# Batch 0's tail loads moved from ScalarE's DMA queue to SyncE's, in a fused attention and MLP-mixer kernel

## The chip, the core and the metric

The kernel runs on one core of a Trainium2 chip. The metric is the device time of one launch in microseconds (us), lower being better; it is given as the median of several runs. A profile of one of the executions is used for everything that is said about single instructions. "Queue" below means the instruction queue of an engine from which DMAs are issued: SyncE's (SP) or ScalarE's (ACT).

## The reference

Two blocks follow each other. The first is a linear attention without softmax, with 8 batches, 8 heads, 576 positions and a head size of 64; the second is a mixer over positions and channels with model width 512 and hidden width 2048. Everything goes in and out as float32.

```python
kv  = einsum('bhsd,bhse->bhde', k, v)            # 64x64 per head
out = einsum('bhsd,bhde->bhse', q, kv)
rms = sqrt(mean(out*out, axis=-1) + 1e-6)
x   = (out / rms * g_norm)                       # then heads joined: [8, 576, 512]

a1  = alpha1 * x + beta1
tok = einsum('ts,bsd->btd', w_tok, a1)           # 576x576 over positions
u   = x + lam * tok
a2  = alpha2 * u + beta2
ch  = maximum(a2 @ w_ch1, 0) @ w_ch2             # 512 -> 2048 -> 512
y   = u + lam * ch
```

## The kernel before

The kernel is one long straight program for all engines. A small planner in the kernel's own Python (`Prog`) writes its order. Every operation is handed to `P.op` with a cost for each engine that could run it, what it reads and writes, and a priority `pri` (smaller is more urgent). `schedule` (L105) then plays the program through with these costs and fixes which engine does what and in which order; `synchronize` and `emit` turn this into instructions and semaphore waits. An operation with `kind="L"` is a load: loads start strictly in the order of their priority, and among equals in the order in which they were written (`in_order`, L132). The planner believes that each load takes its `dma_us` one after the other on a single pipe, plus 2.0 us (L244 to L246). When TensorE has nothing to do in the plan before the first channel matmul, the planner fills in a dummy matmul on the tile `hot` (`dummy`, L290; L931).

Each batch has 576 positions, handled as 512 "main" positions (four chunks of 128) and a "tail" of 64. So q, k and v of one batch come in two ways:

- `load_main` (L499) brings 1 MB, the 512 main positions of all heads, into one of six staging buffers `st`, in pieces of 1 KB that are contiguous in memory. For batch 0, v is brought as two halves of four heads each.
- `load_tail` (L509) brings the last 64 positions of all heads, 128 KB in pieces of 256 B, into `kvft` (k in its lower half of the partitions, v in the upper) or `qft`.

`round_in` (L530) casts what has come into the matmul's type: the mains into `qr`, `kr` and `vr`, the tails into `krt`, `vrt` and `qrt` (L399 on ACT or L400 on DVE; all casts go through one helper). `kv` (L587) multiplies k by v: for batch 0 it does the four main chunks of heads 0 to 3, then those of heads 4 to 7, with the tail's chunk (c = 4, tiles `vrt` and `krt`, L598) last in each sum, so no sum of k times v is complete without the tails. `qtr` (L629) transposes q; L580 is its matmul for the mains, L635 for the tail of batch 0. `norm_first` (L711) is the attention of batch 0: matmuls L723 and L732 give its outputs transposed, ACT squares them (L726, L735), and 40 matmuls with two output columns each add the squares up (L717). The same line L580 then also computes the output with g applied.

`token_weights` (L981) transposes w_tok (L996), after POOL has cast it; `token_sums` (L1007, L1014) and `tok` (L764, L771) follow, then `ut` (L799) and the channel matmuls `ch1` (L838) and `ch2` (L858), which fill the rest of the program. While batch b is in its channel matmuls, the loads, attention and token mixing of later batches are woven in.

All loads are issued by SP, with the exception of batch 0's three tails and of six small parameter vectors (L884 to L891). Those are issued by "AQ", which the planner treats as a queue of its own and which in fact is ACT's instruction queue. The loads' order in `load(0)` is q, k, v first half, v second half (SP), then the tails of q, k, v (ACT's queue); after them SP goes on with w_tok (L893, L896), the four loads of w_ch1 (L1029) and batch 1.

Of the kernel before, what the change touches and what calls it, by code (L numbers as in the profile page):

```python
# [402 lines left out]
def bass_transnormer_attn__then__resmlp_affine_kernel(  # L403
# [15 lines left out]
    with ExitStack() as stack:  # L419
# [3 lines left out]
        def sb(name, shape, dt):  # L423
            return stack.enter_context(nc.sbuf_tensor(name, shape, dt))
# [14 lines left out]
        kvft = sb("kvft", [128, NH, DH], F32)  # L439
        qft = sb("qft", [128, NH, DH], F32)  # L440
# [58 lines left out]
        def load_main(n, src, b, eng, pri, parts=1):  # L499
            i = held[n, b] = stage()  # L500
            nh = NH // parts
            for x in range(parts):
                P.op({eng: 0.6}, lambda e, _, x=x: e.dma_start(
                    st[:, i].rearrange("p (h r) -> p h r", h=NH)[:, nh * x:nh * x + nh],
                    src[b, nh * x:nh * x + nh, 0:512, :].rearrange("h (p c) d -> p h (c d)", c=4)),
                    w=[("st", i, 2 * x // parts + y) for y in range(2 // parts)], dma_us=2.8 / parts,
                    pri=pri, kind="L")

        def load_tail(n, tile, src, b, lo, eng, pri):  # L509
            key = n + "ft" + (str(b % 2) if n == "q" else "")  # L510
            P.op({eng: 0.4}, lambda e, _: e.dma_start(
                tile[lo:lo + 64, :, :], src[b, :, 512:576, :].rearrange("h s d -> s h d")),
                w=[key], dma_us=0.9, pri=pri, kind="L")

        def load(b, pri):
            P.tag = "load.%d" % b
            aq = "AQ" if b == 0 else "SP"
            load_main("q", q, b, "SP", pri)
            load_main("k", k, b, "SP", pri)
            load_main("v", v, b, "SP", pri, 2 if b == 0 else 1)  # L520
            if b == 0:
                load_tail("q", qft, q, 0, 0, aq, pri)
            load_tail("k", kvft, k, b, 0, aq, pri)
            load_tail("v", kvft, v, b, 64, aq, pri)
            if b % 2 == 0 and b:
                load_tail("q", qft, q, b, 0, aq, pri)
            if b % 2 == 0 and b or b == 1:
                load_tail("q", qft, q, b | 1, 64, aq, pri)

        def round_in(b, pri):  # L530
            P.tag = "round_in.%d" % b
# [348 lines left out]


        load(0, -1000)
        for j, src in enumerate((moe_lam, moe_alpha1, moe_beta1)):
            P.op({"AQ": 0.3}, lambda e, _, j=j, s=src: e.dma_start(  # L884
# [3 lines left out]
            pri=-1100)  # L888
        for j, src in enumerate((moe_alpha2, moe_beta2)):
# [5 lines left out]
            pri=-800, kind="L")  # L895
# [15 lines left out]
             pri=-999)  # L911
        P.op(D, lambda e, _: e.tensor_copy(out=identr[:], in_=ident[:]), r=["ident"], w=["identr"],
             pri=-999)
# [155 lines left out]
        tok(0, -390)  # L1069
        ut(0, -390)  # L1070
        load(1, -190)
        round_in(1, -195)
        for key in [("sqt", i) for i in range(5)] + ["e1", "whi"]:
# [9 lines left out]
        for b in range(NB):  # L1083
            B = 100.0 * b
            more, more2 = b + 1 < NB, b + 2 < NB
            n0 = len(P.ops)
            ch1(b, B, 35)
            if first[0] is None:
                first[0] = P.ops[n0]
            if more2:  # L1090
                load(b + 2, B + 12)
            if more:
                norm(b + 1, B + 1)
                tok(b + 1, B + 36)
                if more2:
                    round_in(b + 2, B + 40)
                ut(b + 1, B + 45)
            if more2:
                kv(b + 2, B + 55)
                qtr(b + 2, B + 60)  # L1100
            ch2(b, B + 40, 55)
# [32 lines left out]
```

## Time and profile before

The median is 398.33 us over four runs (397.03 to 399.62). The profiled execution took 398.92 us; its span from first to last instruction is 397.0 us, so 1.9 us lie around the span.

| | before |
|---|---|
| span | 397.0 us |
| mean granted TensorE clock | 0.953 |
| TensorE matmul (PE) busy | 378.2 us, 95% |
| VectorE (DVE) busy | 232.2 us, 58% |
| ScalarE (ACT) busy | 173.8 us, 44% |
| GpSimd (POOL) busy | 81.6 us, 21% |
| moved by DMA on SP's queue | 47.08 MB in 45760 packets |
| moved by DMA on ACT's queue | 0.40 MB in 1608 packets |

How to read the views used below. The *chain of waits* follows the last instruction back to what released each step; a line gives start, length and what it was. The *waits* add up how long an engine sat idle for which releaser, as total, number and longest. The *timeline* gives start, length, engine, line, operation, `out<-in`, shape and count of merged instructions, and in brackets the idle time ahead of them and its releaser. The *table by windows* gives for each stretch of time the busy time of each engine with its number of instructions in brackets, the granted TensorE clock (1.00 is full), the share of DMA time and GB/s. In the names, `ps` is the accumulator memory, PE a matmul and PEld its weight load. "To landing" is the time from issuing a DMA to the release of what waits for it.

### The profile page before, as it was taken

Reading aid. Unit: us, or ns where it says so; the run is one execution under the profiler, and the core shown is the slowest. Engines: PE = TensorE matmul, PEld = TensorE weight load, DVE = VectorE, ACT = ScalarE, POOL = GpSimd, SP = SyncE. Lnnn points to the kernel's source line nnn. Section 1 sums busy time; section 2 is a strip of 40 time slices with the busy share of each in tenths; the row PEclk is TensorE's granted clock in tenths of the full one; section 3 lists DMA queues with packets and bytes.
Section 4 is the critical chain, followed back from the end, with each engine's and each line's share of the span. In section 5 each row is a group of like instructions: output and inputs, shape, how many; then the busy total and the mean of one; then the engine's idle time right before and its main releaser. Section 6 shows DMA issues by size and latency. Waiting matters only on the chain.

```text
span 397.0 us, 5549 instructions
## 1 busy us (share of the span) xinstructions
PE 378.2 (95%) x2240; PEld 234.6 (59%) x2271; DVE 232.2 (58%) x383; ACT 173.8 (44%) x300; POOL 81.6 (21%) x61
## 2 busy tenths in 40 slices
PE   8789997999989999899999999999999999999994
PEld 4469554646878556545686566555775554547641
DVE  6340689796698839954893669374826482710021
ACT  3332763784597225631574126612662147106500
POOL 5210248152016004300350022201420133000000
PEclk9865598999999999999999999999999999999998
DMA  8995698999792912740100011002000210020021
GB/s 248 325 382 173 151 364 267 242 278 308 220 278 83 288 54 75 228 124 35 72 2 2 26 54 53 0 2 79 28 2 0 79 54 0 2 79 28 0 79 54
DMA packets 47393, 47.83 MB, mean 120 GB/s; under 512 B 13885, under 2 KB 38469, under 8 KB 47240
## 3 DMA queue, kind: packets, MB, share of 16 engines
q1 hardware_dynamic: 45760, 47.08, 37.8%
q10 hardware_dynamic: 1608, 0.40, 0.5%
q8 instruction: 18, 0.29, 0.3%
q14 instruction: 7, 0.06, 0.1%
HBM read 38.04 MB, written 9.44 MB: 120 GB/s over the span
## 4 chain that ended last, share of the span: by engine, by line
PE 85%; DVE 7%; DMA 4%; issue 1%; ACTq 1%; ACT 1%
PE ps L858 31%; PE ps L838 29%; PE ps L771 11%; PE ps L584 4%; DMA kvft<-in_v_dram 4%; PE ps L598 2%; PE ps L717 2%; PE ps L799 2%; DVE vr L400 1%; DVE yn L698 1%; PE ps L580 1%; DVE ht L824 1%; PE ps L996 1%; DVE small L686 1%; DVE kr L400 1%
## 5 line engine op out<-in xcount | busy, mean ns | idle before, releaser
L838 PE MATMUL ps<-a2t,w 128*128 128x320 bf16 (+1 forms) x759 | 145.1, 331 | 3.7 <-ACT ht L823 2.4
L858 PE MATMUL ps<-w,ht 128*128 128x512 bf16 x561 | 137.5, 381 | 0.5
L838 PEld LDWEIGHTS ps<-a2t,w 128*128 128x128 bf16 x768 | 73.3, 98 | 44.9 <-ACT ht L823 2.9
L823 ACT ACTIVATE ht<-ps 128x512 bf16<-128x512 f32 (+1 forms) x111 | 72.0, 649 | 54.0 <-PE ps L838 53.4
L858 PEld LDWEIGHTS ps<-w,ht 128*128 128x128 bf16 x576 | 54.7, 98 | 59.5
L704 POOL TENSOR_TENSOR xm<-yn,g_bc 128x512 f32<-128x512 f32 x28 | 45.0, 1606 | 186.2 <-DVE yn L698 185.6
L866 DVE TENSOR_TENSOR xm<-ps,xm 128x512 f32<-128x512 f32 x32 | 22.1, 690 | 56.2 <-PE ps L858 54.5
L779 DVE TENSOR_TENSOR xm<-ps,xm 128x512 f32<-128x512 f32 x32 | 21.8, 690 | 40.7 <-PE ps L771 39.4
L771 PE MATMUL ps<-rt,wt 128*128 128x512 bf16 x155 | 41.8, 390 | 0.3
L684 ACT ACTIVATE sq<-ps 128x512 f32<-128x512 f32 (+1 forms) x35 | 20.7, 592 | 47.8 <-PE ps L584 47.5
L598 PE MATMUL ps<-vr,kr 128*128 128x128 f32 (+1 forms) x128 | 36.9, 382 | 2.9 <-DVE vr L400 2.9
L808 ACT ACTIVATE a2t<-ps,cols 128x512 bf16<-128x512 bf16 (+1 forms) x16 | 12.4, 826 | 47.6 <-PE ps L799 47.6
L584 PE MATMUL ps<-kvc,qt 128*128 128x128 f32 x112 | 32.9, 387 | 0.0
L686 DVE TENSOR_REDUCE small<-sq 128x8 f32<-128x512 f32 (+1 forms) x35 | 23.7, 676 | 10.3 <-ACT sq L684 10.1
L584 PE MATMUL ps<-identr,qr 128*128 128x128 f32 x112 | 29.6, 362 | 0.0
L598 PEld LDWEIGHTS ps<-vr,kr 128*128 128x128 f32 x128 | 26.1, 214 | 5.0 <-DVE vr L400 4.8
L701 DVE TENSOR_TENSOR rt<-yn,ge 128x512 bf16<-128x512 f32 x28 | 26.7, 954 | 0.4
L771 PEld LDWEIGHTS ps<-rt,wt 128*128 128x128 bf16 x160 | 15.8, 100 | 18.5 <-issue 1.6
L698 DVE TENSOR_TENSOR yn<-ps,small 128x512 f32<-128x512 f32 (+1 forms) x35 | 24.0, 685 | 0.5
L584 PEld LDWEIGHTS ps<-kvc,qt 128*128 128x128 f32 x112 | 22.3, 199 | 2.3
L584 PEld LDWEIGHTS ps<-identr,qr 128*128 128x128 f32 x112 | 21.3, 200 | 0.6
L399 ACT ACTIVATE qt<-ps 128x512 fp32r<-128x512 f32 x25 | 14.8, 595 | 7.0 <-PE ps L584 6.9
(122 smaller groups left out, 371.0 us busy)
## 6 DMA issues: line engine op xcount, KB each, us to landing
st<-in_q_dram SPq DMA_DIRECT2D x8, 1024.0 KB, 5.9
st<-in_k_dram SPq DMA_DIRECT2D x8, 1024.0 KB, 8.3
st<-in_moe_w_ch_dram SPq DMA_DIRECT2D x8, 1024.0 KB, 12.7
out_dram<-xm SPq DMA_DIRECT2D x32, 256.0 KB, 2.3
st<-in_v_dram SPq DMA_DIRECT2D x7, 1024.0 KB, 10.7
ht<-in_moe_w_tok_dram SPq DMA_DIRECT2D x1, 1152.0 KB, 13.4
st<-in_v_dram SPq DMA_DIRECT2D x2, 512.0 KB, 11.0
out_dram<-xtl SPq DMA_DIRECT2D x8, 128.0 KB, 2.3
```

The lines of the kernel that those rows point to most:

```text
L584: return e.matmul(t.flat()[:, 128 * pr:128 * pr + 128], a(), m(), start=start, stop=stop)
L598: return e.matmul(t.flat()[:, at:at + w], a, m, start=(c == 0), stop=(c == 4))
L686: P.op({"DVE": dve_us(512)}, lambda e, _: e.tensor_reduce(out=small[rows, s4], in_=sq[rows, s2], axis=AX.X, op=ALU.add), r=[("sq", s2)], w ...
L698: P.op({"DVE": dve_us(512)}, lambda e, _: e.tensor_tensor(out=yn[rows, s3, :].rearrange("p (r h d) -> p r h d", r=4, h=2), in0=heads(t, b, ...
L701: P.op({"DVE": dve_us(512), "POOL": pool_us(512)}, lambda e, _: e.tensor_tensor(out=rto, in0=yn[rows, s3, :], in1=ge1[rows, :], op=ALU.mul ...
L704: P.op({"POOL": pool_us(512)}, lambda e, _: e.tensor_tensor(out=hview(x), in0=hview(yn[rows, s3, :]), in1=g_bc[rows, None, :].to_broadcast ...
L771: return e.matmul(t.flat(), wt[:, sc, col:col + 128], rt[:, sc, :] if sc < 4 else rtt[:], start=(sc == 0), stop=(sc == 4))
L779: P.op({"DVE": dve_us(512)}, lambda e, _: e.tensor_tensor(out=x, in0=t.flat(rows), in1=x, op=ALU.add), r=[t, xkey(b, c)], w=[xkey(b, c)], ...
L823: return e.activation(dst, src(), ACT.Relu)
L838: return e.matmul(o, w1[:, dj, 128 * fj:128 * fj + 128], m, start=(dj == 0), stop=(dj == 3))
L858: P.op({"PE": 0.216}, lambda e, _: e.matmul(t.flat(), ht[:, fj, 128 * c:128 * c + 128], w2[:, fj, :], start=(fj == 0), stop=(fj == 15)), r ...
L866: P.op({"DVE": dve_us(512)}, lambda e, _: e.tensor_tensor(out=x, in0=t.flat(), in1=x, op=ALU.add), r=[t] + keys, w=keys, pri=p - 2)
```

## The change

Batch 0's three tail loads go to SP's queue, like those of all other batches. Because loads start in the order in which they are written, they are issued after v's second half and ahead of w_tok. Their order among themselves becomes k, v, q instead of q, k, v. Nothing else is edited; the planner runs again on the changed list.

```diff
         def load(b, pri):
             P.tag = "load.%d" % b
-            aq = "AQ" if b == 0 else "SP"
             load_main("q", q, b, "SP", pri)
             load_main("k", k, b, "SP", pri)
             load_main("v", v, b, "SP", pri, 2 if b == 0 else 1)
-            if b == 0:
-                load_tail("q", qft, q, 0, 0, aq, pri)
-            load_tail("k", kvft, k, b, 0, aq, pri)
-            load_tail("v", kvft, v, b, 64, aq, pri)
-            if b % 2 == 0 and b:
-                load_tail("q", qft, q, b, 0, aq, pri)
+            load_tail("k", kvft, k, b, 0, "SP", pri)
+            load_tail("v", kvft, v, b, 64, "SP", pri)
+            if b % 2 == 0:
+                load_tail("q", qft, q, b, 0, "SP", pri)
             if b % 2 == 0 and b or b == 1:
-                load_tail("q", qft, q, b | 1, 64, aq, pri)
+                load_tail("q", qft, q, b | 1, 64, "SP", pri)
```

## The prediction

> **What bounds the kernel now.** I read the page first: TensorE is busy for 378.2 of 397.0 us, and after 80 us for 307.34 of 317, so only the first 80 us hold much that a load could change. Then I read the chain of waits from 0 to 60 us, since all that the diff touches happens there.
>
> ```profile
> 4.50 15.07 DMA kvft<-in_v_dram
> 19.59 1.43 DVE vrt L400
> ...
> 21.07 0.74 PE ps L598 x4
> 21.80 0.67 PE ps L635 x4
> 22.47 2.00 PE ps L723 x4
> 24.48 2.00 PE ps L948 x2
> 26.48 1.80 PE ps L717 x8
> ```
>
> Batch 0's v tail, issued by ACT's queue at 4.50, lands at 19.57. Its cast ends at 21.0, and only then can the last four matmuls of k times v run. From there the chain is TensorE almost without a break until 52.9. But 15.07 us on the chain is not what can be won: TensorE worked through most of it. The timeline of TensorE shows how much was idle:
>
> ```profile
> 14.89 1.30 PE L948 MATMUL ps<-xm,ones 1*128 1x512 f32 x2
> 16.12 1.22 PE L598 MATMUL ps<-vr,kr 128*128 128x256 f32 x8
> 17.18 1.04 PE L931 MATMUL ps<-hot 128*128 128x512 bf16 x4
> 21.07 0.74 PE L598 MATMUL ps<-vrt,krt 128*128 128x256 f32 x4 [2.85 <-DVE vrt L400]
> ```
>
> The main chunks of k times v are issued by 17.18; what follows until 21.07 is four dummies and 2.85 us of idleness. Third, the table by windows, cut at the places where the granted clock changes (columns: PE, PEld, DVE, ACT, POOL, clock, DMA share, GB/s):
>
> ```profile
> 8.47:11.88 3.41, 2.17 (x12) 1.22 (x10) 0.90 (x3) 1.63 (x3) 0.00 (x0) 1.00 1.15 284
> 11.88:15.29 3.41, 3.41 (x13) 3.01 (x14) 1.54 (x5) 1.23 (x2) 0.00 (x0) 0.50 1.12 337
> 15.29:18.70 3.41, 2.93 (x14) 1.39 (x13) 0.99 (x3) 0.60 (x1) 1.59 (x2) 1.00 1.02 317
> 18.70:22.12 3.42, 1.05 (x8) 0.92 (x8) 1.87 (x4) 0.59 (x4) 2.71 (x3) 1.00 1.05 384
> 22.12:25.53 3.41, 3.41 (x9) 1.87 (x8) 1.39 (x4) 2.46 (x7) 0.00 (x0) 0.50 1.05 387
> ...
> 28.95:32.36 3.41, 3.41 (x17) 3.41 (x18) 0.00 (x0) 0.00 (x0) 0.00 (x0) 0.50 1.08 349
> ...
> 46.01:49.43 3.42, 3.42 (x12) 1.78 (x11) 2.89 (x5) 3.42 (x7) 0.00 (x0) 0.50 1.28 251
> 49.43:52.84 3.41, 3.41 (x17) 1.57 (x16) 2.20 (x5) 1.21 (x2) 0.00 (x0) 1.00 1.04 306
> ```
>
> The window in which TensorE waits for the tail (1.05 of 3.42 us busy) is followed at 22.12 by half clock, and it stays half for 27.3 us, through a stage that TensorE bounds. The wait may therefore cost more than its own length.
>
> **Part 1: when the v tail lands.** The trace's packet records say why it is late. From 9 to 13 us each microsecond holds about 225 packets of 1 KB (k and v mains, SP's queue) and about as many of 256 B (tails, ACT's queue): the two queues take turns packet by packet. From 14 to 16 us the partner is w_tok with packets of 9216 B, and both kinds fall to about 40 per us. The v tail's small packets each wait behind a large one and the last starts at 18.9. In one queue the tails lie ahead of w_tok. By the same records the mains ran at about 330 KB per us before the tails joined; at 8 us 1.30 MB of them were left, 3.9 us at that rate, so their last packet starts at about 11.9 instead of 13.7, and v's second half lands at about 13.1 (it took about 1.1 us from there before, to 14.8). A tail behind a main on SP's queue is seen in batch 2: issued at 69.59, 70.25 and 70.92 and landed 6.3, 6.4 and 6.5 us later, so 0.7 to 0.8 apart. So k tail 13.8, v tail 14.6, q tail 15.3: the v tail is 5.0 us sooner. Its cast took 1.42 us; krt's cast of the same size took 0.41, and POOL was casting w_tok (18.38 to 20.7) during the long one. At 0.41 it is ready by about 15.2.
>
> **Part 2: what of this counts.** With the same order on TensorE the main chunks still end at 17.18, perhaps 0.2 sooner, since k also lands a little sooner but the ACT casts ahead of it set the pace. The next late thing is TensorE itself. Gain: 21.07 − 17.18 = 3.9 us, of which about 1 is dummies that the planner places into its own idle time; if it keeps them all the gain is 2.9. The planner believes the v tail 0.9 us sooner than before, so I take them as gone: 3.9, ends 2.9 and 4.3. The q tail moves the other way: 15.3 instead of 11.4, plus a cast of 0.41. Its matmuls L635 come after the k·v tail, at about 17.9, so 2.2 us of cover remain; without cover it would cost its lateness.
>
> **Part 3: the issues.** ACT loses three issues of 0.73, 0.64 and 0.67 us at 3.06 to 5.17; it waited for q until 6.32 anyway, so 0. SP gains three of about 0.65, ahead of w_tok, of w_ch1 and of batch 1: w_tok is issued at about 7.0 instead of 4.95. Here a rule of the Trainium skill speaks against the change: DMA: Bandwidth & Descriptors, "Issuing engines are not separate DMA queues", says that a second issuing engine does save sequencer time. By it 2.0 us could be lost on everything queued behind. By the row, w_tok took 13.4 us from issue to landing with DMA share at 1.0 and above from 5 to 34 us: it queues for bandwidth, and the bytes ahead of it are no more than before. I take 0, and at worst 2.0 us later landings: w_tok about 20.4, POOL's casts (3.1 us) done by 23.5, first used by L996 at 35.97 before, about 29 after. w_ch1's first load lands at 21.2 and is cast at 34.88; batch 1's q lands at 33.9, cast at 49.60. All covers are 5 us or more.
>
> **Part 4: the clock.** Without the wait, the k·v tail, L635 and L723 follow from 17.2 on, so the window 18.70 to 22.12 holds L723, L948 and the first L717 instead of 1.05 us of work. The fall to half should come at least a window later. By the skill (TensorE: Matmul & The Clock Gate, "What's actually happening") about 3.4 us of sustained activity release the throttle. By that rule the first full window at 22.12 would have done so, and work without the idle gap would never be throttled: the 27.3 us would then shrink by up to half, 13.6 us. The rows say otherwise: windows from 22.12 to 46 are full of PE (3.41 of 3.41) and stay at 0.50. L717's matmuls have two output columns and L948's one input row; they keep the profile's PE busy and evidently do not count. So I let the clock fall in L717's stage again, one window later: 3.4 us at full clock do up to 3.4 us more half-clock work. L717 also waits for ACT's four squares (2.06 us), so I take two thirds, 2.4 us; ends 0 and 13.6, nearest the row of L717.
>
> **Part 5: the new plan.** The list scheduler runs again, and small shifts could change orders anywhere. After 80 us TensorE has 9.7 us of idle in all; I bound this at plus or minus 2 us and take 0.
>
> **Sum.** 3.9 + 2.4 = 6.3 us off the profiled 398.92 gives 392.6; the median lies 0.6 below that execution, so 392.0.
>
> **Rivals.**
> - *Only the wait goes*, and the clock falls at the same piece of work: 398.3 − 3.9 = 394.4. For it: 8.47 to 11.88, with 2.17 us of PE busy, was followed by half clock, so a partly filled window may not be enough. Against: 15.29 to 18.70 was not.
> - *The clock holds*: with L723 and L717 at full speed the stage is short enough to reach real matmuls. 392.0 − 11.2 is the floor, 381; I put it at 383. The full windows at half clock speak against it.
> - *The tails do not come sooner*, because SP cannot issue them: the two v halves took 1.5 us each to issue and one w_ch1 issue took 5.33, so SP is held up while much is outstanding. Two such holds ahead of the v tail: 4.95 + 2 × 5.33 = 15.6, plus the shortest landing of a tail, 2.8, is 18.4, plus the cast 18.8: only 2.3 of the 3.9 us, and nothing of the clock, if the new plan also loses 1 us: 397.
> - *Slower, through DVE beside POOL.* At 57.87 two casts of v (L400) took 5.43 us while POOL ran its multiplies by lam (L1048, 10.36 us for four); a cast of equal shape took 0.68 at 50.95. TensorE then waited, and half clock followed from 63.08 to 66.50. Each further cast that the new plan puts beside POOL costs about 2.0 us if TensorE waits for it, and one more half-clock window 1.7. It decides from a loss of 8.3 us on: four casts and one window are 9.7, giving 401.7. For it: the order there is the planner's free choice. Against: four more is most of what POOL's stretch can hold.
>
> **How the numbers follow.** Forecast 0.42; only the wait 0.27; clock holds 0.11; tails not sooner 0.10; slower 0.10. A measurement of this kernel can tell about 0.5%, 2 us, from no change. The first three are faster by more than that: 0.80. The fourth is within it, 0.10, and the last is slower, 0.10. The range runs from 385, the forecast with 7 us of the clock's unknown, to 397.5, which takes in the wait alone with its lower end, 2.9, and 2 us of a bad plan; out of it are most of the clock case and the slower case, 0.2 in all.
>
> **What would show it.** Right: `kvft<-in_v_dram` landing at 14 to 15.5; the k·v tail matmuls at about 17.2 with no wait for vrt; w_tok landing within 2 us of 18.4; clock 1.00 in the window that ends near 22, then 0.50 during L717. Wrong: an SP issue of the tails later than 12 us; TensorE waiting at L635 for the q tail or at L996 for w_tok; more DVE time of L400 in 57 to 70 us; or 0.50 already ahead of L723.

## The result, and the profile after

The changed kernel takes 383.34 us (median of 12 runs, 381.54 to 394.01) against 398.88 us for the kernel before (median of 17 runs); the ratio is 0.9617, 95% interval 0.9585 to 0.965. That is 15.5 us faster where 6.3 were forecast, and below the range. In 5 of the 18 executions of the changed kernel in this study TensorE's clock was at half for 26 to 31 us and the time 391 to 394 us; this and every later ratio leaves out executions that lie over 1.5% above the fastest of their kernel, as those five do. The profiled execution took 382.95 us, its span is 381.0 us, its mean granted clock 0.982 (before: 397.0 and 0.953). Lines of the kernel after the edit are smaller by 3 than before: L595 is the old L598, L632 the old L635, L714 the old L717, L720 the old L723, L945 the old L948.

The chain of waits from 0 to 55 us of the changed kernel no longer has a tail on it; the same three steps stand as follows (start, length, what):

```profile
16.53 0.56 PE ps L595 x3
17.09 0.56 PE ps L632 x4
17.65 0.89 PE ps L720 x3
```

The tails of k times v, which ran at 21.07, are done by 17.1, and the first attention matmul follows at 17.65 instead of 22.47. In TensorE's timeline the wait for vrt has gone:

```profile
13.99 1.22 PE L595 MATMUL ps<-vr,kr 128*128 128x256 f32 x8
15.10 0.38 PE L595 MATMUL ps<-vrt,krt 128*128 128x256 f32 x1
15.41 1.12 PE L945 MATMUL ps<-xm,ones 1*128 1x512 f32 x2
16.46 0.63 PE L595 MATMUL ps<-vrt,krt 128*128 128x256 f32 x3
```

Main chunks and tails now follow each other; the new plan has put a broadcast (L945) in between. No dummies stand there any more. The table by windows of the changed kernel, in steps of 3.41 us; its granted clock falls at 22.73 and is back at 32.97, so the cuts at 22.51 and 32.75 lie 0.2 us ahead of the changes (PE, PEld, DVE, ACT, POOL, clock, DMA share, GB/s):

```profile
15.68:19.10 3.42, 3.42 (x18) 2.31 (x18) 2.88 (x8) 2.45 (x8) 0.92 (x2) 1.00 1.01 324
19.10:22.51 3.41, 3.41 (x32) 3.41 (x31) 0.99 (x1) 2.43 (x5) 2.60 (x3) 1.00 1.05 387
22.51:25.92 3.41, 3.41 (x20) 3.41 (x18) 0.00 (x0) 0.00 (x0) 0.00 (x0) 0.53 1.05 384
25.92:29.34 3.42, 3.25 (x20) 2.50 (x22) 1.99 (x5) 2.12 (x5) 0.45 (x1) 0.50 1.05 382
29.34:32.75 3.41, 3.25 (x16) 2.23 (x16) 1.71 (x4) 3.20 (x6) 2.10 (x2) 0.50 1.09 350
32.75:36.16 3.41, 3.41 (x22) 1.88 (x21) 2.80 (x5) 1.68 (x3) 0.00 (x0) 0.97 1.09 348
```

Half clock lasts three of these windows, 10.2 us, where it lasted 27.3 before. The two short stretches at half clock of the kernel before, 11.88 to 15.29 and 63.08 to 66.50, are absent too. A second profile of the changed kernel (383.86 us) has the same 10.2 us in two stretches, 18.95 to 22.36 and 25.78 to 32.60, so the place is not fixed.

An account can be made from two numbers of each run. If the clock is either full or half, the time at half is 2 × (1 − mean clock) × span: 37.3 us before, 13.7 after. If TensorE bounds that time, half of it is lost. The span less that half is 378.4 before and 374.1 after. So 11.8 us of the 16.0 in the two profiles are the clock, and 4.3 are the wait and the rest.

One profile is one execution, and that of the kernel before lies high. In the 57 other executions of it whose clock is on record, the time at half was 22.6 to 43.7 us, median 30.0; in the 18 of the changed kernel the median is 13.0. By these medians the clock is worth some 8.5 us of 14, not 11.8 of 16. The stretch at 11.88 in particular is not the change's doing: the profile "gap filled" below has the same program and the same transfers up to there and does not have it.

### The profile page after: what moved, and what is told of

It is laid out like the page before. It is cut to its first block, busy times and chain, and to the rows that moved or that the text cites. A ratio compares the mean times of both kernels' runs of the same rounds, so it can differ in the third digit from the quotient of the medians.

```text
span 381.0 us, 5547 instructions
## 1 busy us (share of the span) xinstructions
PE 367.2 (96%) x2238; PEld 227.5 (60%) x2270; DVE 229.8 (60%) x384; ACT 173.1 (45%) x298; POOL 82.3 (22%) x62
## 4 chain that ended last, share of the span: by engine, by line
PE 83%; DVE 10%; DMA 2%; ACT 2%; issue 1%; SPq 0%
PE ps L855 30%; PE ps L835 28%; PE ps L768 11%; PE ps L581 4%; PE ps L595 3%; DMA st<-in_k_dram 2%; PE ps L796 2%; DVE rt L698 2%; DVE w L1045 2%; PE ps L714 1%; PE ps L577 1%; DVE small L683 1%; DVE ht L821 1%; DVE yn L695 1%; DVE kr L400 1%
## 5 line engine op out<-in xcount | busy, mean ns | idle before, releaser
L835 PE MATMUL ps<-a2t,w 128*128 128x320 bf16 (+1 forms) x760 | 143.4, 329 | 4.3 <-DVE ht L821 2.7
L820 ACT ACTIVATE ht<-ps 128x512 bf16<-128x512 f32 (+1 forms) x107 | 69.5, 650 | 50.1 <-PE ps L835 49.5
L768 PE MATMUL ps<-rt,wt 128*128 128x512 bf16 x155 | 40.1, 380 | 0.3
L595 PE MATMUL ps<-vr,kr 128*128 128x128 f32 (+1 forms) x128 | 34.7, 365 | 0.0
L581 PE MATMUL ps<-kvc,qt 128*128 128x128 f32 x112 | 32.4, 384 | 0.0
L683 DVE TENSOR_REDUCE small<-sq 128x8 f32<-128x512 f32 (+1 forms) x35 | 23.5, 676 | 9.4 <-ACT sq L681 9.3
L698 DVE TENSOR_TENSOR rt<-yn,ge 128x512 bf16<-128x512 f32 x28 | 28.1, 1009 | 0.4
L595 PEld LDWEIGHTS ps<-vr,kr 128*128 128x128 f32 x128 | 24.6, 200 | 1.1 <-DVE vr L400 0.8
L399 ACT ACTIVATE qt<-ps 128x512 fp32r<-128x512 f32 x26 | 15.5, 596 | 8.2 <-PE ps L581 7.8
```

What stands on the lines that cost most here:

```text
L581: return e.matmul(t.flat()[:, 128 * pr:128 * pr + 128], a(), m(), start=start, stop=stop)
L595: return e.matmul(t.flat()[:, at:at + w], a, m, start=(c == 0), stop=(c == 4))
L683: P.op({"DVE": dve_us(512)}, lambda e, _: e.tensor_reduce(out=small[rows, s4], in_=sq[rows, s2], axis=AX.X, op=ALU.add), r=[("sq", s2)], w ...
L698: P.op({"DVE": dve_us(512), "POOL": pool_us(512)}, lambda e, _: e.tensor_tensor(out=rto, in0=yn[rows, s3, :], in1=ge1[rows, :], op=ALU.mul ...
L768: return e.matmul(t.flat(), wt[:, sc, col:col + 128], rt[:, sc, :] if sc < 4 else rtt[:], start=(sc == 0), stop=(sc == 4))
L820: return e.activation(dst, src(), ACT.Relu)
```

## The experiments

The theory T1: the tails' earlier landing removes TensorE's idle gap, and with the gap goes a long stretch of half clock. The rival T2: the edit made the planner write another order, and that order is what is faster. Both could be tried apart, because an op's queue can be changed after the plan is made and before the semaphores are set. The kernel before ran beside each set of runs, with a median of 396.98 to 397.63 us. The edits are shortened to the lines that matter.

**The old plan with the tails on SP, and the new plan with the tails on ACT's queue.**

```diff
 # kernel before
         P.schedule()
+        for o in [o for o in P.sequence if o.kind == "L" and o.eng == "AQ"]:
+            o.eng = "SP"
         P.synchronize()
```

```diff
 # changed kernel
         P.schedule()
+        at = [P.sequence.index(o) for o in tails]      # tails: k, v, q of batch 0
+        for i, o in zip(at, (tails[2], tails[0], tails[1])):
+            P.sequence[i] = o
+            o.eng = "AQ"
         P.synchronize()
```

Expected of the first:

> The order of every compute engine is that of the kernel before, fixed after its planner has run; only batch 0's three tail loads are issued from SP's queue (in the old order q, k, v) instead of ACT's. Theory T1, the transfers and the clock that follows from the idle gap: the v tail lands by about 15.5 us, TensorE doesn't idle ahead of k times v's tail, and half clock comes one window later or more; time 384 to 389, most of the 15 us. Theory T2, the new plan: with the old order only the wait itself is won, 393 to 395, since the 40 two-column matmuls still stand in one block and keep the clock at half up to the token mixing.

Measured: 389.62 us, ratio 0.983 (0.9730 to 0.9931), against 396.98 for the kernel before beside it. Expected of the second:

> The order of every compute engine is that of the changed kernel; only batch 0's three tail loads are issued from ACT's queue again, in the old order q, k, v. T1: the v tail lands at about 19.5 us again, TensorE idles some 4 us, half clock follows the idle window; 395 to 400, nearly all the gain gone. T2: the wait comes back (about 4.5 us) but the new order keeps its part; 387 to 390.

Measured: 400.07 us, ratio 1.0115 (1.0064 to 1.0167), at the upper end of what T1 expected. That is within 2% of the kernel before, and its median is 3.1 us above that of the kernel before beside it (396.98), so the new order alone wins nothing. The transfers alone give 7.4 us, about half of the gain, just above what T1 expected and well below T2's times. T2 falls as the sole cause. Something of it remains, since the two parts together give more than the sum: the new order is good only when the tail is early.

What the order adds shows in two places. The half clock of the old plan on SP lasts 17.1 us (22.8 to 39.8), not 10.2. Its TensorE hardly waits for the tail, and its first and last windows at half clock are these:

```profile
16.30 0.74 PE L598 MATMUL ps<-vrt,krt 128*128 128x256 f32 x4 [0.52 <-DVE vrt L400]
```

```profile
22.80:26.20 3.40, 3.40 (x17) 3.40 (x17) 0.00 (x0) 1.29 (x3) 0.00 (x0) 0.50 1.04 383
...
36.40:39.80 3.40, 3.40 (x13) 1.92 (x12) 2.74 (x4) 3.38 (x8) 0.00 (x0) 0.50 1.21 259
```

And the old plan keeps the stall at batch 1's v casts. DVE's timeline of the old plan on SP:

```profile
48.35 5.44 DVE L400 CAST vr<-st 128x1024 fp32r<-128x1024 f32 x2
```

and of the changed kernel:

```profile
44.20 1.28 DVE L400 CAST vr<-st 128x1024 fp32r<-128x1024 f32 x2
```

The same two casts take 1.28 us where the new order puts them ahead of POOL's multiplies by lam, and 5.44 beside them. In the old plan on SP TensorE waits there and loses the clock once more:

```profile
50.10:53.50 3.40, 1.06 (x5) 0.49 (x5) 3.40 (x2) 1.02 (x2) 3.24 (x3) 1.00 1.05 373
53.50:56.90 3.40, 3.06 (x11) 2.07 (x11) 3.34 (x4) 0.60 (x1) 3.32 (x2) 0.50 1.05 314
```

The two profiles differ by 6.5 us (387.5 and 381.0). Their times at half clock, 23.3 and 13.7, account for 4.8 of it. Most of it arises early: the first channel matmul starts at 57.97 in the kernel before, 48.20 in the old plan on SP and 44.07 in the changed kernel. Which part of the new order keeps the clock up is not tested.

**The wait kept, only the idleness filled.** In the kernel before, 13 dummies stand in the gap:

```diff
         P.schedule()
+        first_tail = min(P.sequence.index(o) for o in KVT)   # KVT: tail matmuls of k times v
+        dummies(first_tail, 13)                              # hot x hot into a free bank
         P.synchronize()
```

> The kernel before, with its plan and its tails on ACT's queue, and 13 more dummy matmuls of 512 columns put on TensorE just ahead of the four tail matmuls of k times v; they add no needed work. The wait for the v tail stays whole, only the idleness goes. T1: the clock stays full past 22 us and the first part of the attention of batch 0 runs at full speed; 3 to 8 us are won, 390 to 395. If idleness is not what takes the clock down: 398 to 399, no change, or up to 1 us slower through dummies that outlast the wait.

Measured: 393.97 us, ratio 0.9932 (0.9873 to 0.999): the smallest gain that T1 expected, 3.0 us below the median of the kernel before beside it. Useless work made the kernel slightly faster. Its table by windows:

```profile
16.90:20.30 3.40, 2.84 (x14) 1.08 (x11) 0.29 (x1) 0.00 (x0) 2.30 (x3) 1.00 1.06 304
20.30:23.70 3.40, 3.08 (x14) 2.02 (x14) 2.11 (x7) 2.31 (x8) 0.74 (x1) 1.00 1.05 388
23.70:27.10 3.40, 3.40 (x29) 3.08 (x28) 1.39 (x2) 0.74 (x2) 0.00 (x0) 1.00 1.05 386
27.10:30.50 3.40, 3.40 (x18) 3.32 (x18) 0.00 (x0) 1.56 (x3) 0.00 (x0) 0.55 1.06 366
```

The k·v tail still comes at 20.61, half a microsecond from where it was, but the clock holds to 27.4 instead of 22.12, and half clock lasts 17.1 us instead of 27.3. Half of the 10.2 us is 5.1; the profiled spans differ by 5.0 (397.0 and 392.0). Over all executions of that set of runs the median time at half clock is 22.8 us with the gap filled, 30.0 in the kernel before and 23.3 in the old plan on SP. So with the order held, filling the gap saves as much half clock as the early tail does: idleness took the clock down, not the lateness of the data.

**The wait put back into the changed kernel, idle and filled.**

```diff
         P.schedule()
+        P.sequence[first_tail].deps.add(wtok_last)     # the load of w_tok's last rows
+        dummies(first_tail, 16)                        # in the second kernel only
         P.synchronize()
```

> The changed kernel with one wait more: the first tail matmul of k times v also waits for the last part of w_tok (lands near 18.7 us in the changed kernel's profile), so TensorE idles about 3.5 us with all tails landed. T1: the idle window brings the half clock back early; 3.5 us for the wait and 4 to 9 us for the clock, 391 to 396. T2: only the wait's own length, 386.5 to 387.5.

> The changed kernel with the same added wait as the one before (the first tail matmul of k times v also waits for the last part of w_tok), and 16 dummy matmuls of 512 columns ahead of the waiting matmul; they add no needed work. The wait is as long, but TensorE doesn't idle through it. T1, the clock follows idleness: about 3.5 to 5 us above the changed kernel, 386 to 389, against the 398.7 of the idle wait. If the lateness itself costs more (work behind it, loads, other engines): near 395 or above.

Measured: idle 398.71 us, ratio 0.999 (0.9912 to 1.0067), somewhat more than even T1 expected; filled 392.06 us, ratio 0.9861 (0.9826 to 0.9897), 3 us more than expected. TensorE's timeline with the idle wait:

```profile
13.71 1.22 PE L597 MATMUL ps<-vr,kr 128*128 128x256 f32 x8
19.85 0.58 PE L597 MATMUL ps<-vrt,krt 128*128 128x256 f32 x1 [4.93 <-DMA ht<-in_moe_w_tok_dram]
```

and with the filled one:

```profile
14.83 3.63 PE L933 MATMUL ps<-hot 128*128 128x512 bf16 x16
19.09 0.38 PE L597 MATMUL ps<-vrt,krt 128*128 128x256 f32 x1 [0.63 <-DMA ht<-in_moe_w_tok_dram]
```

One wait of 5 us brings back everything that the change had gained. Filling it returns about 6 us of that: the profiled spans are 396.9 and 391.5, the times at half clock 33.3 and 21.9, and half of that difference is 5.7. The expectation for the filled kernel missed because I counted only the wait: its trace has half clock in stretches from 21.6, 28.4 and 55.7 us, and 21.9 us in all are 8.2 more than in the changed kernel. Over the executions the medians are 34 us idle and 18.7 filled, against 13.0 in the changed kernel, so here the filling saves most of the lost clock but not all of it.

**One queue, but the tails behind w_tok.**

```diff
         P.schedule()
+        for o in tails:
+            P.sequence.remove(o)
+        i = P.sequence.index(wtok_last) + 1
+        P.sequence[i:i] = tails
         P.synchronize()
```

> The changed kernel's plan and SP alone as the queue, but the three tails are issued behind w_tok's two parts. If the order in front of w_tok is what brings the gain, the tails land at about 18.5 to 20 us, k times v waits some 4 to 5 us and the half clock comes early: 395 to 400. If the single queue as such brings it (no packets of a second queue between the mains'): below 388.

Measured: 399.1 us, ratio 1.0021 (0.9993 to 1.0048). All of the gain is gone. Its first tail matmul waits as with two queues:

```profile
18.86 0.58 PE L595 MATMUL ps<-vrt,krt 128*128 128x256 f32 x1 [3.73 <-DVE vrt L400]
```

So a single queue is no gain in itself. What counts is that the tails' packets lie ahead of w_tok's.

**Can the rest of the half clock be won?** Dummies of 384 columns between the two-column matmuls (9 of them), and in a second kernel also dummies of 128 columns between the transposes. In a third, three dummies of 512 columns ahead of each of the two groups of main chunks of k times v and of its tail; in a fourth the first and third together.

```diff
         P.schedule()
+        for at in two_column_matmuls[1:19:2]:          # fill_sums; ts is their accumulator bank
+            after(at, matmul(ts[:, 128:512], hot, hot x 3))
+        for at in (kv_main[0], kv_main[8], kv_tail[0]): # fill_kv
+            dummies(P.sequence.index(at), 3)
         P.synchronize()
```

> The changed kernel with 9 dummy matmuls of 384 columns (no needed work) strewn between the matmuls with two output columns (L714 in the changed kernel). At full clock they cost 9 times 0.16, 1.4 us. T1 with its part on low activity: if two-column matmuls don't count as activity, the dummies keep the clock up through that stage, half-clock time falls from 10.2 us to 0 to 7 us, and the time is 378 to 382. If the clock falls all the same, 383 to 385.

> As the one with 9 dummies, and 9 or more further dummies of 128 columns between the transposes of w_tok (L993 in the changed kernel). Cost at full clock 1.4 us and about 0.5 us. If transposes too don't count as activity, this one keeps the clock up where the other loses it later: 377 to 380; otherwise as the other plus 0.5 us.

> The changed kernel with 9 dummy matmuls of 512 columns (no needed work): three ahead of the first main chunks of k times v, three ahead of the second, three ahead of its tail. They cost at most 9 times 0.22, 2.0 us, less what falls into idle time. If the long half clock of some executions begins because a window full of one-row matmuls (L945) and few others counts as idle, no execution is near 393 any more, and all lie at 381.5 to 388. If it begins for another reason: some near 394 to 395 as before.

> The changed kernel with the 9 dummies of 512 columns around k times v and the 9 dummies of 384 columns between the two-column matmuls. If both stages lose the clock only for want of counted activity: half clock for under 8 us in all executions, all of them at 379 to 382. If the early dummies don't help: two groups again, near 380 and near 395.

> The changed kernel once more, for runs beside the next three on one chip. 381.5 to 386 us with the clock at half for 7 to 15 us, as measured; some executions near 393, with the clock at half for about 30 us.

| | median, us | ratio to before | 95% interval | at half clock, us, in its executions |
|---|---|---|---|---|
| changed kernel again | 383.37 | 0.9627 | 0.9572 to 0.9682 | four of 7 to 12, two of 26 and 30 |
| dummies at the sums | 379.93 | 0.9532 | 0.9491 to 0.9573 | four of 1 to 3, three of 31 to 32 |
| also at the transposes | 388.32 | 0.9565 | 0.9518 to 0.9612 | three of 2 to 7, three of 26 to 33 |
| dummies around k times v | 384.03 | 0.9671 | 0.962 to 0.9722 | six of 10 to 16 |
| at both places | 381.87 | 0.9597 | 0.9545 to 0.965 | four of 1.5 to 3, two of 28 |

The dummies at the sums do what was expected of counted activity: four executions keep nearly the full clock and take 378.9 to 379.9 us, though they do 9 matmuls more. But three others lose it early, and take 394.6 to 394.7. The profile of that kernel is of such an execution. Its windows:

```profile
12.47:15.88 3.41, 3.41 (x15) 1.74 (x14) 2.39 (x5) 1.04 (x3) 1.28 (x1) 1.00 1.18 298
15.88:19.30 3.42, 3.42 (x12) 2.73 (x12) 2.74 (x8) 2.04 (x6) 1.17 (x2) 0.53 1.00 324
```

and the matmuls with one input row in TensorE's timeline of the same execution:

```profile
12.62 1.12 PE L950 MATMUL ps<-xm,ones 1*128 1x512 f32 x2
...
14.94 1.12 PE L950 MATMUL ps<-xm,ones 1*128 1x512 f32 x2
```

The first window is full by the profile and yet followed by half clock. Two broadcasts lie in it (L950 there is L945 of the changed kernel): 1.12 us, and 0.94 of the second's. I read this as a window in which too little counts. Dummies around k times v should then cure it. With them alone no execution of six was above 386.52, but with both kinds two of six still were at 395. So why some executions lose the clock at 16 us and others don't stays open; where the clock's windows fall against the program differs from profile to profile (one begins at 12.27 in the changed kernel's, one at 12.47 in this), which fits, but isn't shown to be the cause. The profile with both kinds of dummies is of an execution that kept the clock from 6.9 to 375.5 us. No version beats the changed kernel in all its executions.

**The old plan on SP, with dummies at the sums.**

> The old plan with its tails on SP's queue (389.5 without dummies), and the 9 dummies of 384 columns between the two-column matmuls. If what the new plan adds is mostly the clock, this one comes within 2 to 4 us of the changed kernel with the same dummies: 381 to 384. If the new order itself is worth more: 386 to 389.

Measured: 389.0 us, ratio 0.9791 (0.9735 to 0.9847), as without them (0.983). It can't tell what it was meant to: the dummies didn't hold the clock there, since its executions had half clock for 17 to 28 us against 16 to 25 without. Inconclusive.

**The profiles by one account.** Those without dummies at the sums or around all of k times v. Span, time at half clock by the formula above, and the span less half of that, in us:

| profile | span | at half clock | span less half of it |
|---|---|---|---|
| before | 397.0 | 37.3 | 378.4 |
| gap filled | 392.0 | 23.5 | 380.2 |
| new plan, tails on ACT's queue | 395.4 | 32.4 | 379.2 |
| tails behind w_tok | 397.2 | 35.0 | 379.7 |
| changed, idle wait | 396.9 | 33.3 | 380.3 |
| changed, filled wait | 391.5 | 21.9 | 380.5 |
| old plan, tails on SP | 387.5 | 23.3 | 375.9 |
| changed | 381.0 | 13.7 | 374.1 |
| changed again | 381.9 | 11.5 | 376.2 |

The last column falls into two groups: 378 to 381 where the k·v tail waits, 374 to 376 where it doesn't. The wait is worth some 4 us, whatever the plan; the medians over all executions say 3.6 (379.5 before, 375.9 changed). Most of what else differs follows the middle column. Over the 18 executions of the changed kernel a straight line through span and time at half clock has a slope of 0.54 to 0.55, near the half that a TensorE-bound stage would give; over the 57 of the kernel before it is only 0.37, so the account is rough.

## Why the prediction was wrong

The sum had three terms. The runs that hold the planner's order allow each to be measured, in us:

| term | forecast | in the profiles | by medians of executions |
|---|---|---|---|
| the wait (Part 2) | 3.9 | 2.5 | 3.4 |
| the clock, order held (Part 4) | 2.4 | 7.0 | 3.4 |
| the new plan (Part 5) | 0 | 6.5 | 6.3 |

The first two rows compare the kernel before with the old plan on SP, the last one that with the changed kernel, whose median comes from other sets of runs. By medians the edit with its order held gained 7.4 us (2.8 to 10.7 by the interval of its ratio), near the 6.3 forecast. The step that failed is the new plan at 0; the clock's term was too small as well, by 1.0 us in the medians and 4.6 in the profiles.

**What bounds the kernel: right.** The place, the length of the idle gap and the stage at half clock behind it were what the change acted on.

**Part 1, landings: right.** k, v and q tail landed at 13.7, 14.6 and 15.5 (forecast 13.8, 14.6, 15.3); the last main packet started at 12.2 (11.9). The sharing of the two queues is gone from the packet records: 340 main packets per us from 8 to 10 us.

**Part 2, the wait: right in size.** The four dummies went in the changed kernel, as assumed. The q tail was hidden: DVE waited 0.5 us for it, and L632 started at 17.02 right behind the k·v tail.

**Part 3, issues: right in effect, wrong in time.** SP was held up more than I had it: w_tok was issued at 9.74, not 7.0, since each tail took 1.4 to 1.7 us to issue while mains were still outstanding. It landed at 18.6 nevertheless, 0.3 us later than before. The sequencer time was spent, but cost nothing here.

**Part 4, the clock: mis-sized.** "So I let the clock fall in L717's stage again, one window later": that half happened, at 22.73. "3.4 us at full clock do up to 3.4 us more half-clock work … I take two thirds, 2.4 us": that was too little. In the profile with the order held, half clock begins only 0.65 us later than before (22.77), yet ends 9.6 us earlier (39.84), since TensorE is further on in the program at every point; half of the 10.2 us saved is 5.1. The rest of the 7.0 is mostly the stretch at 11.88, which the change did not cause. With the new plan the clock's part is 8.5 us by medians and 11.8 in the profiles.

The reading behind it, that two-column and one-row matmuls do not count, is not enough either. This window of the kernel before holds 2.52 us of L1014 and 0.93 of L580, and the clock stayed at half after it:

```profile
42.60:46.01 3.41, 3.38 (x13) 1.68 (x13) 1.47 (x2) 1.67 (x4) 0.96 (x1) 0.50 0.56 178
```

In the changed kernel the window from 29.55 to 32.97 held 1.22 us of the same matmuls (L1011), 1.39 of L577 and 1.58 of transposes (L993), and the clock came back. What brings it back stays open.

**Part 5, the new plan: the step that failed.** "I bound this at plus or minus 2 us and take 0." The new order is worth 6.3 to 6.5 us once the tail is early, and nothing without that. Three quarters of it in the profiles is again clock. The bound came from TensorE's idleness after 80 us, where little changed: TensorE idles 8.8 us there in the old plan on SP and 9.1 in the changed kernel. The new order acts in the first 80 us, the stage that the forecast itself had named as the one that counts, and mostly through the clock. The mechanism of the slower rival, casts on DVE beside POOL, was real (5.44 against 1.28 us) but went the other way: the new plan took the two casts out from beside POOL.

**The rival "the clock holds"** gave the time, 383, at a chance of 0.11. That its number fits is in good part luck: the clock did not hold, it came back earlier, and the last 6 us came from the new order, which that rival does not contain. I set it aside because TensorE was full in windows at half clock, from which I took that nothing would restore the clock before the token mixing. Such windows did stay at half (two of those up to 46.01 held 3.19 and 3.38 us, not 3.41), but they didn't show how little of that work would be left. And I had bounded the term from 0 to 13.6 and then ended the range at 385, which cut off just that upper part.

## What to carry to other kernels

A wait of a few microseconds on TensorE is priced by what its clock does afterwards, up to the place where it comes back. Count the time at half clock from span and mean clock, take half of it as the stake, and let the range reach all of it when the start and the end of the half clock can both move. Take that time from several executions: one profile of the kernel before showed 37 us where the median was 30. Where a list scheduler writes the order, a changed queue is two changes; hold the order fixed and try each. Here the second was worth some 6 us, and only together with the first.

A small transfer that is needed early belongs ahead of the large ones in the same queue. In a second queue it got about as many packets per us as the first, and beside packets of 9216 B its own of 256 B fell from about 220 to 40 per us.

## What was not expected of the hardware

Nine more matmuls at the sums gave the shortest executions of the study, 378.9 to 379.9 us; thirteen more in the gap of the kernel before took 3.0 us off its median. A window that the profile shows full of TensorE work can still be followed by half clock: 19.10 to 22.51 in the changed kernel, 3.41 of 3.41 us busy, with 2.84 us of two-column matmuls in it. And the same program can lose the clock in one execution and not in another: the changed kernel's executions had half clock for between 7 and 31 us, those of the kernel before for between 23 and 44.
